# Expert rows loaded as 32x32 blocks and transposed by VectorE, zeros written at run-time addresses

## The chip, the cores and the metric

The kernel runs on one core of a Trainium2 chip. The time is the device time of one launch in microseconds (us). TensorE (PE) multiplies, VectorE (DVE), ScalarE (ACT) and GpSimd (POOL) do the rest, and SyncE (SP) issues most of the DMAs.

## The reference

Two stages follow one another. The first is a linear attention with a state (batch 4, 8 heads, 768 steps, head size 48):

```python
for t in range(S):
    kt, vt, rt = (k[:, :, t], v[:, :, t], r[:, :, t])
    cur = np.einsum('bhd,bhe->bhde', u[None] * kt, vt)
    y[:, :, t] = np.einsum('bhd,bhde->bhe', rt, state + cur)
    state = w[None, :, :, None] * state + np.einsum('bhd,bhe->bhde', kt, vt)
```

Its output, as 3072 tokens of 384 numbers, goes into a mixture of experts with 4 groups of 4 experts. Each token goes to one expert, the best of its best group:

```python
h = np.maximum(xg[mask_e] @ w1[g, e], 0.0)      # 384 -> 1024
ye = h @ w2[g, e]                               # 1024 -> 384
out[tok_idx] = (g_w[mask_g][mask_e] * e_w[mask_e])[:, None] * ye
```

All data is 32-bit float.

## The kernel before

**Attention stage.** The tokens are cut into 24 tiles of 128 (6 chunks of the sequence for each of 4 batches), and a loop over steps `s` runs a pipeline written out by hand: step `s` transposes tile `s` (`turn`), computes the scores of tile `s - 1`, the values of tile `s - 2`, brings tile `s - 3` back to rows (`back`) and finishes the routing of tiles further behind. The term of the token's own key (`own`, `own_sum`, `own_values`) runs on POOL, VectorE and ACT; `own_values(n)` makes eight scalings on ACT, which `back(n)` needs. The order of the instructions on each engine is the order of the code in this stage, since it is scheduled manually. The wait for data, on the other hand, is worked out by the framework: it sees a DRAM tensor that is addressed through a register as one whole.

**Routing.** After each group of tiles `route` picks an expert for every token and a place in that expert's region of the DRAM tensor `xs_dram` (named `x_sorted` in the profile). Each row there has 384 numbers, a token number and a gate. `rows` scatters 128 rows with an indirect DMA from POOL (L410). A region is longer than it has tokens, and the expert stage reads a fixed number of rows (`SLOTS`), so rows behind the last token must read as zeros. `zero_places` (L321) writes zeros over the first 256 places of every region in steps 3, 5, 7 and 9, in four DMAs from ACT's queue, ahead of all scatters.

**Expert stage.** After two thirds of the tiles `pick_first` names the two experts with most tokens; the others are sorted later (`order_i`). The experts run in that order, each with its number of slots, 256 for the first to 173 for the last. An item is one expert's work, the first expert being cut into two items. For item `i`: `load_rows` (L472) loads the rows from `xs_dram` in DMAs of up to 128 rows; `columns` (L483) transposes them on TensorE by blocks of 128x128 into PSUM and copies them to `xe` on VectorE (L486); `up` (L506) multiplies by w1, ACT applies relu (L510); `down` (L520) multiplies by w2; `rows_out` transposes back, multiplies by the gate and scatters to the output from POOL (L534). Two places hold weights, so `load_expert` (L430, L431) for w1 waits until `up` of two experts earlier is done, and for w2 until its `down` is done.

SP issues its DMAs strictly in order. In this stage the code of one item reads, cut to SP's share:

```python
up(i, 0); up(i, 2); up(i, 4); up(i, 6)
expert = expert_of(order_i[0:1, e : e + 1], (SP,))   # a register load
load_rows(i + 2, expert, nc.sync)
down(i, 0); columns(i + 1); down(i, 1); down(i, 2)
weights[e] = load_expert(expert, e % 2)
```

The DMAs of SP and ACT use eight semaphores in turn, so a DMA is not issued before the one eight places ahead of it has landed. Tiles of rows have three buffers.

Of the kernel before, what the change touches and what calls it, by code (L numbers as in the profile page):

```python
# [34 lines left out]
def kernel(  # L35
# [35 lines left out]

    x_dram = nc.dram_tensor("x_rows", [N, DM], FP32).ap()

    RG = N + P
    xs_dram = nc.dram_tensor("x_sorted", [GE * RG, XW], FP32).ap()
    w1f = moe_w1.rearrange("g e (ko p) f -> (g e) p ko f", p=P)
    w2f = moe_w2.rearrange("g e (fo p) d -> (g e) p fo d", p=P)
# [11 lines left out]
    def cst(shape, name, dtype=FP32):  # L89
        return const.tile(shape, dtype, name=name)  # L90
# [199 lines left out]

    is_first = cst([P, GE], "is_first")
    first_i = cst([P, 2], "first_i", I32)
    sorted_key = cst([P, GE], "sorted_key")
    order_i = cst([P, GE], "order_i", I32)

    def token_keys(i):

        pc = bank([P, 2, GE], "pc")
        nc.tensor.matmul(pc[:, 0, :], lhsT=ones, rhs=cum[:, i, :], start=True, stop=True)
        nc.vector.scalar_tensor_tensor(  # L300
            out=pc[:, 1, :], in0=pc[:, 0, :], scalar=float(GE), in1=key_base, op0=OP.mult, op1=OP.add
        )
        return pc[:, 1, :]

    def number_of(out, key_i):
        nc.vector.tensor_scalar(
# [3 lines left out]
    def pick_first():  # L310
        keys = token_keys(FOUR * B)
        top = cst([P, 8], "top")
        nc.vector.max(out=top, in_=keys)
        nc.vector.tensor_scalar(out=is_first, in0=keys, scalar1=top[:, 1:2], scalar2=None, op0=OP.is_ge)
        nc.vector.scalar_tensor_tensor(
            out=is_first, in0=keys, scalar=top[:, 0:1], in1=is_first, op0=OP.is_equal, op1=OP.add
        )
        nc.vector.tensor_copy(first_i, top[:, 0:2])
        number_of(first_i, first_i)

    def zero_places(j):  # L321

        regions = xs_dram.rearrange("(e n) w -> n e w", e=GE)
        part = CAP // 4
        nc.scalar.dma_start(out=regions[part * j : part * (j + 1)], in_=spread(nothing[0:part, :], 1, GE))

    NA = 1 + G

# [95 lines left out]
        ),  # L424
    ]

    def load_expert(e, i, queue=nc.sync):

        w1, w2 = places[i]
        queue.dma_start(out=w1, in_=w1f[bass.ds(e, 1)].rearrange("a p k f -> (a p) k f"))  # L430
        queue.dma_start(out=w2, in_=w2f[bass.ds(e, 1)].rearrange("a p k f -> (a p) k f"))  # L431
        return w1, w2

    def transposed(x, dst):

# [8 lines left out]


    ITEMS = [(0, 0, P), (0, P, SLOTS[0])] + [(e, 0, SLOTS[e]) for e in range(1, GE)]
    by_expert = xs_dram.rearrange("(e n) w -> e n w", e=GE)
    pools = {0: early}
    weights, xgs, xes, keys_of, hTs, yo = {}, {}, {}, {}, {}, {}

    def width(i):
        return ITEMS[i][2] - ITEMS[i][1]
# [7 lines left out]
    def room(i):  # L460
        return P if i == 0 else CAP

    def load_rows(i, expert, queue):
        shape = [P, room(i) // P, XW]
        if i < 3:
            xg = pools[0].tile(shape, FP32, name=f"xg_{i}")
        else:
            xg = pools[1].tile(shape, FP32, tag="xg", bufs=3, name="xg")
        xgs[i] = xg
        for j, n in enumerate(parts(i)):  # L470
            a = ITEMS[i][1] + P * j
            queue.dma_start(  # L472
                out=xg[0:n, j, :], in_=by_expert[bass.ds(expert, 1), a : a + n, :].rearrange("a n w -> (a n) w")
            )

    def columns(i):
        xg, w = xgs.pop(i), width(i)
        xe = xes[i] = item_tile(i, [P, KO, room(i)], "xe")
        for ks in (range(0, KO),) if KO * w <= 512 else (range(0, 2), range(2, KO)):
            px = bank([P, len(ks), w], "px")  # L480
            for q, ko in enumerate(ks):
                for j, n in enumerate(parts(i)):
                    nc.tensor.transpose(  # L483
                        px[:, q, P * j : P * j + n], xg[0:n, j, P * ko : P * (ko + 1)], ident[0:n, 0:n]
                    )
            nc.vector.tensor_copy(xe[:, ks[0] : ks[-1] + 1, 0:w], px)  # L486
        ids = item_tile(i, [P, 2], "ids", U32, bufs=4)
        gates = item_tile(i, [P, 2], "gates", bufs=4)
        for j, n in enumerate(parts(i)):
            nc.vector.tensor_scalar(  # L490
                out=ids[0:n, j : j + 1], in0=xg[0:n, j, DM + ROW_ID : DM + ROW_ID + 1], scalar1=float(N),
                scalar2=None, op0=OP.add,
            )
            nc.vector.tensor_copy(gates[0:n, j : j + 1], xg[0:n, j, DM + ROW_GATE : DM + ROW_GATE + 1])
        keys_of[i] = ids, gates

    def up(i, f):
# [186 lines left out]
    def expert_of(number, engines):  # L684
# [2 lines left out]
            skip_runtime_bounds_check_because="four bits of a whole number",  # L687
        )

    LAST = 5  # L690
    for s in range(NT + LAST):
        pieces = todo.pop(s, [])

        def run(when):
            for at, part in pieces:
                if at == when:
                    part()

        if s % 2 == 0 and s // 2 + 2 < NP:
            load_pair(s // 2 + 2)  # L700
        if s == 1:
            load_small()
        if s in (3, 5, 7, 9):
            zero_places(s // 2 - 1)
        if s == FOUR * B + 6:
            pieces.append(("last", pick_first))
        if s == FOUR * B + 7:
            first = expert_of(first_i[0:1, 0:1], (SP,))
            weights[0] = load_expert(first, 0)
        if s == FOUR * B + 9:  # L710
            load_rows(0, first, nc.sync)
            second = expert_of(first_i[0:1, 1:2], (SP,))
            weights[1] = load_expert(second, 1)
        if s == FOUR * B + 10:
            columns(0)
        run("first")
        if s < NT:
            turn(s)
            if s % 2 == 1 and s // 2 + 1 < NP:
                if s > 1:  # L720
                    scale_k(s // 2 + 1, nc.gpsimd)
                own(s // 2 + 1)
        for n in range(NT):
            if s == max(n + 1, 2):
                own_values(n)
        run("choice")
        if 0 <= s - 4 < NT:
            rows_T(s - 4)
        n = s - 5
        if 0 <= n < NT:  # L730
            row_logits(n)
        if 0 <= s - 3 < NT:
            back(s - 3)
        if 0 <= s - 2 < NT:
            values(s - 2)
        if s % 2 == 0 and 0 < s // 2 < NP:
            own_sum(s // 2)
        run("last")
        if 0 <= s - 1 < NT:
            scores(s - 1)  # L740
        if s == 1:
            own_sum(0)

        if s in (0, 3):
            backwards(s // 3 + 1, nc.scalar)
        if s in (1, 4):
            turned(s // 3 + 1)
            powers(s // 3 + 1, nc.scalar)
        if s == 3:
            span_decay()  # L750
        if s == 4:
            check_decay()
        if n in ROUTED:
            choice, before, gate, place, rows = routing(n)
            T = ROUTED[n]
            if n >= NT - B - 1:
                choice()
                todo.setdefault(s + 1, []).extend(
                    [("last", part) for part in (before, gate, place)]
                    + [("last", lambda i=i, rows=rows: rows(i)) for i in range(T)]  # L760
                )
            else:
                todo.setdefault(s + 1, []).append(("choice", choice))
                todo.setdefault(s + 2, []).extend([("first", before), ("last", gate), ("last", place)])
                for i in range(T):
                    at = s + 3 + (i // 2 if n == FOUR * B - 1 else i)
                    todo.setdefault(at, []).append(("last", lambda i=i, rows=rows: rows(i)))
        if s == FOUR * B + 10:
            up(0, 0)
# [12 lines left out]
    nc.vector.match_replace(out=keys, in_to_replace=sorted_key[:, 0:8], in_values=keys, imm_value=-1.0)  # L782
    nc.vector.max(out=sorted_key[:, 8:16], in_=keys)
    nc.vector.tensor_copy(order_i, sorted_key)
    number_of(order_i, order_i)
    over = cst([1, GE], "over")
    nc.vector.tensor_sub(over, sorted_key[0:1, :], most[0:1, :])
# [17 lines left out]
    with ExitStack() as moe:  # L805
        pools[1] = moe.enter_context(tc.tile_pool(name="moe", bufs=2, reuse_waits="tile"))
        with tc.manual_schedule(engines={mybir.EngineType.PE}):
            columns(1)
            for i in range(1, len(ITEMS)):
                up(i, 0)  # L810
                up(i, 2)
                if i > 1:
                    rows_out(i - 1)
                up(i, 4)
                up(i, 6)
                e = ITEMS[i][0] + 2
                if e < GE:
                    expert = expert_of(order_i[0:1, e : e + 1], (SP,))
                    load_rows(i + 2, expert, nc.sync)
                down(i, 0)  # L820
                if i + 1 < len(ITEMS):
                    columns(i + 1)
                down(i, 1)
                down(i, 2)
                if e < GE:
                    weights[e] = load_expert(expert, e % 2)
# [224 lines left out]
```

## Time and profile before

| what | value |
|---|---|
| median of 3 runs | 477.19 us (476.6 to 482.25) |
| the profiled execution | 479.58 us |
| its span, first to last instruction | 477.9 us |
| mean granted TensorE clock | 0.973 |
| TensorE busy | 449.7 us (94%) |
| VectorE, ACT, POOL busy | 159.5, 139.0, 129.5 us |
| DMA traffic | 86.24 MB, 112024 packets, mean 180 GB/s |

The span is that of the profiled execution. "Busy" is the time in which an engine runs instructions; an engine that waits or only issues DMAs is not busy. A line of a group gives the source line, engine, operation, output and inputs, shapes and count, then the total and the mean duration, and then the idle time before these instructions and who ended it. A line of the waits gives who waited, for whom, the total in us, the number of waits and the longest. A line of a timeline gives start and length in us, and in brackets the idle time before it. A line of a DMA issue gives the size and the median time from issue to landing.

### The profile page before, as it was taken

How to read it: one execution, taken by the hardware profiler on the slowest of the kernel's cores; microseconds unless marked ns; L12 is line 12 of the kernel's file. 1: busy time of each engine (PE TensorE's matmuls, PEld its weight loads, DVE VectorE, ACT ScalarE, POOL GpSimd, SP SyncE). 2: the span in 40 equal slices, each digit the busy share in tenths (PEclk: the TensorE clock that was granted, in tenths of full speed). 3: DMA queues.
4: the chain of work that ended last, by engine and by line, in shares of the span. 5: the costliest groups of instructions: out<-in, count | busy, mean ns of one | idle time of the engine just before them, and what ended most of it. 6: DMA issues, size and time to landing. Idle time of an engine off the chain costs nothing. (4 is left out here: it accounts for less than half of the span.)

```text
span 477.9 us, 9090 instructions
## 1 busy us (share of the span) xinstructions
PE 449.7 (94%) x3623; PEld 430.6 (90%) x3623; DVE 159.5 (33%) x478; ACT 139.0 (29%) x418; POOL 129.5 (27%) x135
## 2 busy tenths in 40 slices
PE   3799999999999898999999999999999999999992
PEld 2598888899999798999999999999999999999991
DVE  5546566877778663010110210110110110111000
ACT  2846553564656321111121111111111111111120
POOL 7834536556564042000010210110120110120011
PEclk9969979999999989999999999999999999999997
DMA  9999999983102994565465754755856765666000
GB/s 176 187 190 228 207 227 202 200 155 77 36 35 69 339 335 132 188 239 168 160 190 182 256 184 153 280 201 156 284 190 198 255 188 199 238 202 236 30 22 26
DMA packets 112024, 86.24 MB, mean 180 GB/s; under 512 B 79633, under 2 KB 103568, under 8 KB 111976
## 3 DMA queue, kind: packets, MB, share of 16 engines
q1 hardware_dynamic: 98920, 68.81, 52.1%
q10 hardware_dynamic: 8432, 7.31, 7.1%
q0 software_dynamic: 4624, 9.48, 5.8%
q8 instruction: 30, 0.49, 0.5%
q14 instruction: 18, 0.15, 0.1%
HBM read 69.79 MB, written 16.12 MB: 180 GB/s over the span
## 5 line engine op out<-in xcount | busy, mean ns | idle before, releaser
L534 POOL DMA_INDIRECT out_dram<-yt,ids x32 | 34.1, 1066 | 255.0 <-DVE yt L532 250.4
L506 PE MATMUL ph<-xe,w 128*128 128x128 f32 (+7 forms) x432 | 72.2, 325 | 0.7 <-DVE xe L486 0.7
L520 PE MATMUL po<-hT,w 128*128 128x128 f32 (+7 forms) x432 | 71.4, 322 | 0.0
L506 PEld LDWEIGHTS ph<-xe,w 128*128 128x128 f32 x432 | 69.0, 194 | 1.2 <-DVE xe L486 0.9
L532 DVE TENSOR_SCALAR yt<-pb,gates 128x384 f32<-128x384 f32 (+15 forms) x32 | 18.3, 611 | 153.4 <-PE pb L530 153.4
L520 PE MATMUL po<-hT,rall 128*128 128x240 f32 (+7 forms) x384 | 68.6, 336 | 0.0
L506 PE MATMUL ph<-xe,kall 128*128 128x240 f32 (+7 forms) x384 | 68.4, 335 | 0.0
L520 PEld LDWEIGHTS po<-hT,w 128*128 128x128 f32 x432 | 67.8, 190 | 0.5
L510 ACT ACTIVATE hT<-ph 128x256 f32<-128x256 f32 (+15 forms) x68 | 33.5, 493 | 112.9 <-PE ph L506 112.9
L520 PEld LDWEIGHTS po<-hT,rall 128*128 128x128 f32 x384 | 65.0, 190 | 0.7
L506 PEld LDWEIGHTS ph<-xe,kall 128*128 128x128 f32 x384 | 64.9, 190 | 0.6
L523 ACT COPY yo<-po 128x128 f32<-128x128 f32 (+15 forms) x51 | 16.3, 320 | 127.7 <-PE po L520 127.7
L564 ACT ACTIVATE dv<-vt,du 128x48 f32<-128x48 f32 x192 | 45.8, 324 | 1.1 <-DVE du L558 1.0
L594 DVE TENSOR_TENSOR am<-pa,later 128x512 f32<-128x512 f32 x48 | 30.9, 685 | 9.0 <-PE pa L589 8.7
L486 DVE COPY xe<-px 128x384 f32<-128x384 f32 (+30 forms) x32 | 14.0, 475 | 53.6 <-PE px L483 53.6
L410 POOL DMA_INDIRECT x_sorted<-xt,place_i x24 | 23.8, 990 | 27.9 <-issue 14.0
L589 PE MATMUL pa<-rT,kT 48*128 48x128 f32 x384 | 29.3, 291 | 0.7 <-DVE xt L646 0.7
L611 PE MATMUL py<-am,vt 128*64 128x128 f32 x384 | 29.2, 290 | 0.7 <-DVE am L594 0.6
L553 POOL TENSOR_TENSOR dg<-rall,kall 128x768 f32<-128x768 f32 x12 | 21.9, 1821 | 28.9 <-DVE du L558 28.9
L548 POOL TENSOR_TENSOR kh<-kall,T 128x768 f32<-128x768 f32 (+1 forms) x12 | 21.4, 1788 | 28.0 <-DMA kall<-in_k_dram 9.7
L611 PEld LDWEIGHTS py<-am,vt 128*64 128x64 f32 x384 | 22.7, 143 | 4.7 <-DVE am L594 1.5
L589 PEld LDWEIGHTS pa<-rT,kT 48*128 48x128 f32 x384 | 24.4, 193 | 2.6 <-DVE xt L646 0.9
(128 smaller groups left out, 469.6 us busy)
## 6 DMA issues: line engine op xcount, KB each, us to landing
w<-in_moe_w_dram SPq DMA_DIRECT2D x16, 1536.0 KB, 6.8
kall<-in_moe_w_dram SPq DMA_DIRECT2D x8, 1536.0 KB, 7.1
rall<-in_moe_w_dram SPq DMA_DIRECT2D x8, 1536.0 KB, 6.8
x_sorted<-nothing ACTq DMA_DIRECT2D x4, 1544.0 KB, 10.2
rall<-in_r_dram SPq DMA_DIRECT2D x12, 384.0 KB, 7.2
vt<-in_v_dram SPq DMA_DIRECT2D x12, 384.0 KB, 6.8
kall<-in_k_dram SPq DMA_DIRECT2D x10, 384.0 KB, 6.4
xg<-x_sorted SPq DMA_DIRECT2D x17, 193.0 KB, 6.2
```

Source lines behind the costliest of these rows:

```text
L410: ins = nc.gpsimd.indirect_dma_start(out=xs_dram, out_offset=bass.IndirectOffsetOnAxis(ap=place_i[:, i : i + 1], axis=0), in_=xt[:, i, :], ...
L506: nc.tensor.matmul(ph[:, q, :], lhsT=w1[:, ko, P * (f + q) : P * (f + q + 1)], rhs=xe[:, ko, 0:w], start=(ko == 0), stop=(ko == KO - 1), s ...
L510: nc.scalar.activation(hTs[i][:, f : f + 2, 0:w], ph, AF.Relu)
L520: nc.tensor.matmul(po, lhsT=w2[:, fo, P * d : P * (d + 1)], rhs=hT[:, fo, 0:w], start=(fo == 0), stop=(fo == FO - 1))
L532: nc.vector.tensor_scalar(out=yt[0:n], in0=pb[0:n], scalar1=gates[0:n, j : j + 1], scalar2=None, op0=OP.mult)
L534: ins = nc.gpsimd.indirect_dma_start(out=out, out_offset=bass.IndirectOffsetOnAxis(ap=ids[0:n, j : j + 1], axis=0), in_=yt[0:n], in_offset ...
L548: engine.tensor_mul(khs[g % (RING - 1)][:, a0:a1, :, 0:D], kts[g % RING][:, a0:a1], spread(T2[m], 1, a1 - a0))
L553: nc.gpsimd.tensor_mul(dg, rts[g % RING][:, :, :, 0:D], kts[g % RING])
L564: nc.scalar.mul(dv[:, h, :], vts[g % (RING + 1)][:, a, h, 0:D], dvs[g][:, a, h : h + 1])
L589: nc.tensor.matmul(pa[e][:, hc, :], lhsT=kT[rows, hc, :], rhs=rT[rows, hc, :], start=True, stop=True, skip_group_check=True,)
L594: nc.vector.tensor_mul(am[:, e], pa[e], spread(later, 1, HP))
L611: nc.tensor.matmul(py[DP * e : DP * (e + 1), hc, :], lhsT=vt[:, a, 2 * hc + e, :], rhs=am[:, e, hc, :], start=(c == 0), stop=True, skip_gr ...
```

## The change

The rows of an expert are no longer loaded as whole rows. Each item's tile is loaded by 12 DMAs, each of which takes 32 columns of all its tokens, in blocks of 32 tokens by 32 numbers (128 bytes at a time), so that each 32x32 block lies at the place where its transpose belongs; VectorE then transposes the blocks in place of TensorE. Token number and gate come with DMAs of their own (`key`). The four early zero fills are gone. In their place `no_tokens` writes zeros behind an expert's last token, at an address made of the count of its tokens, from SP's queue: for the first two experts after step 23 in the code, for every later one ahead of its row loads. Regions become 128 rows longer. The loads of the first two experts' weights are put in another order: w1 of the first, then rows and zeros, then the other three. `own_values(n)` runs one step later for n above 0. The four scatters of the sixteenth tile's group are put into one step.

```diff
-    def zero_places(j):
-        regions = xs_dram.rearrange("(e n) w -> n e w", e=GE)
-        part = CAP // 4
-        nc.scalar.dma_start(out=regions[part * j : part * (j + 1)], in_=spread(nothing[0:part, :], 1, GE))
+    regions = xs_dram.rearrange("(e n) w -> e n w", e=GE)
+    def no_tokens(e, count, rows):
+        for a in range(0, rows, P):
+            n = min(P, rows - a)
+            nc.sync.dma_start(out=xs_dram[bass.ds(e * RG + count + a, n), :], in_=nothing[0:n, :])
...
+        xg, key = xgs[i] = tl([P, KO, room(i)], "xg"), tl([P, room(i) // P, ROW_EXTRA], "key")
+        a, w, rows = ITEMS[i][1], padded(width(i)), regions[bass.ds(expert, 1)]
+        for q in range(P // BL):
+            for ko in range(KO):
+                col = P * ko + BL * q
+                queue.dma_start(
+                    out=xg[BL * q : BL * (q + 1), ko, 0:w].rearrange("t (b d) -> t b d", d=BL),
+                    in_=rows[:, a : a + w, col : col + BL].rearrange("a (b t) d -> t (a b) d", t=BL),
+                )
         for j, n in enumerate(parts(i)):
             queue.dma_start(
-                out=xg[0:n, j, :], in_=by_expert[bass.ds(expert, 1), a : a + n, :].rearrange("a n w -> (a n) w")
+                out=key[0:n, j, :], in_=rows[:, a + P * j : a + P * j + n, DM:XW].rearrange("a n w -> (a n) w")
             )
...
-            px = bank([P, len(ks), w], "px")
-            for q, ko in enumerate(ks):
-                for j, n in enumerate(parts(i)):
-                    nc.tensor.transpose(
-                        px[:, q, P * j : P * j + n], xg[0:n, j, P * ko : P * (ko + 1)], ident[0:n, 0:n]
-                    )
-            nc.vector.tensor_copy(xe[:, ks[0] : ks[-1] + 1, 0:w], px)
+        for ko in range(KO):
+            nc.vector.transpose(xe[:, ko, 0:w], xg[:, ko, 0:w])
...
         if s == FOUR * B + 7:
             first = expert_of(first_i[0:1, 0:1], (SP,))
-            weights[0] = load_expert(first, 0)
-        if s == FOUR * B + 9:
-            load_rows(0, first, nc.sync)
             second = expert_of(first_i[0:1, 1:2], (SP,))
-            weights[1] = load_expert(second, 1)
+            first_tokens = [tokens(first_n[0:1, i : i + 1]) for i in range(2)]
+            load_w1(first, 0)
...
-            if s == max(n + 1, 2):
+            if s == n + 2:
                 own_values(n)
...
+        if s == FOUR * B + 7:
+            load_rows(0, first, nc.sync)
+            no_tokens(first, first_tokens[0], CAP)
+            no_tokens(second, first_tokens[1], CAP)
+            load_w2(first, 0)
+            weights[0], weights[1] = places[0], load_expert(second, 1)
...
-                    at = s + 3 + (i // 2 if n == FOUR * B - 1 else i)
+                    at = s + 3 + (0 if n == FOUR * B - 1 else i)
...
                     expert = expert_of(order_i[0:1, e : e + 1], (SP,))
+                    no_tokens(expert, tokens(order_n[0:1, e : e + 1]), padded(SLOTS[e]))
                     load_rows(i + 2, expert, nc.sync)
```

`tokens` loads a count into a register of SP, and `padded` rounds up to a multiple of 32. `first_n` and `order_n` hold the counts, made by one shift each on VectorE.

More of the change, by code (lines that the diff above doesn't have):

```diff
@@ L72 @@
     x_dram = nc.dram_tensor("x_rows", [N, DM], FP32).ap()
-    RG = N + P
+    RG = N + CAP
     xs_dram = nc.dram_tensor("x_sorted", [GE * RG, XW], FP32).ap()
@@ L292 @@
     first_i = cst([P, 2], "first_i", I32)
+    first_n = cst([P, 2], "first_n", I32)
     sorted_key = cst([P, GE], "sorted_key")
     order_i = cst([P, GE], "order_i", I32)
+    order_n = cst([P, GE], "order_n", I32)
     def token_keys(i):
@@ L303, in token_keys, with tokens_of @@
         return pc[:, 1, :]
+    def tokens_of(out, key_i):
+        nc.vector.tensor_scalar(out=out, in0=key_i, scalar1=4, scalar2=None, op0=OP.logical_shift_right)
     def number_of(out, key_i):
@@ L318, in pick_first @@
         nc.vector.tensor_copy(first_i, top[:, 0:2])
+        tokens_of(first_n, first_i)
         number_of(first_i, first_i)
-    def zero_places(j):
-        regions = xs_dram.rearrange("(e n) w -> n e w", e=GE)
-        part = CAP // 4
-        nc.scalar.dma_start(out=regions[part * j : part * (j + 1)], in_=spread(nothing[0:part, :], 1, GE))
+    regions = xs_dram.rearrange("(e n) w -> e n w", e=GE)
[3 more added lines that the diff above has]
+            nc.sync.dma_start(out=xs_dram[bass.ds(e * RG + count + a, n), :], in_=nothing[0:n, :])
     NA = 1 + G
@@ L425, with load_w1, load_w2, load_expert @@
     ]
[L427 to L432, printed above, removed]
+    def load_w1(e, i):
+        nc.sync.dma_start(out=places[i][0], in_=w1f[bass.ds(e, 1)].rearrange("a p k f -> (a p) k f"))
+    def load_w2(e, i):
+        nc.sync.dma_start(out=places[i][1], in_=w2f[bass.ds(e, 1)].rearrange("a p k f -> (a p) k f"))
+    def load_expert(e, i):
+        load_w1(e, i)
+        load_w2(e, i)
+        return places[i]
     def transposed(x, dst):
@@ L446 @@
     ITEMS = [(0, 0, P), (0, P, SLOTS[0])] + [(e, 0, SLOTS[e]) for e in range(1, GE)]
-    by_expert = xs_dram.rearrange("(e n) w -> e n w", e=GE)
     pools = {0: early}
     weights, xgs, xes, keys_of, hTs, yo = {}, {}, {}, {}, {}, {}
+    BL = 32
     def width(i):
@@ L461, in room, with padded, tl @@
         return P if i == 0 else CAP
+    def padded(n):
+        return -(-n // BL) * BL
     def load_rows(i, expert, queue):
[L464 to L469, printed above, removed]
+        def tl(shape, name):
+            if i < 3:
+                return pools[0].tile(shape, FP32, name=f"{name}_{i}")
+            return pools[1].tile(shape, FP32, tag=name, bufs=3, name=name)
+        xg, key = xgs[i] = tl([P, KO, room(i)], "xg"), tl([P, room(i) // P, ROW_EXTRA], "key")
[7 more added lines that the diff above has]
+                )
         for j, n in enumerate(parts(i)):
-            a = ITEMS[i][1] + P * j
             queue.dma_start(
-                out=xg[0:n, j, :], in_=by_expert[bass.ds(expert, 1), a : a + n, :].rearrange("a n w -> (a n) w")
+                out=key[0:n, j, :], in_=rows[:, a + P * j : a + P * j + n, DM:XW].rearrange("a n w -> (a n) w")
             )
     def columns(i):
-        xg, w = xgs.pop(i), width(i)
+        xg, key = xgs.pop(i)
+        w = padded(width(i))
         xe = xes[i] = item_tile(i, [P, KO, room(i)], "xe")
-        for ks in (range(0, KO),) if KO * w <= 512 else (range(0, 2), range(2, KO)):
-            px = bank([P, len(ks), w], "px")
-            for q, ko in enumerate(ks):
-                for j, n in enumerate(parts(i)):
-                    nc.tensor.transpose(
-                        px[:, q, P * j : P * j + n], xg[0:n, j, P * ko : P * (ko + 1)], ident[0:n, 0:n]
-                    )
-            nc.vector.tensor_copy(xe[:, ks[0] : ks[-1] + 1, 0:w], px)
+        for ko in range(KO):
+            nc.vector.transpose(xe[:, ko, 0:w], xg[:, ko, 0:w])
         ids = item_tile(i, [P, 2], "ids", U32, bufs=4)
@@ L490, in columns @@
             nc.vector.tensor_scalar(
-                out=ids[0:n, j : j + 1], in0=xg[0:n, j, DM + ROW_ID : DM + ROW_ID + 1], scalar1=float(N),
-                scalar2=None, op0=OP.add,
+                out=ids[0:n, j : j + 1], in0=key[0:n, j, ROW_ID : ROW_ID + 1], scalar1=float(N), scalar2=None, op0=OP.add
             )
-            nc.vector.tensor_copy(gates[0:n, j : j + 1], xg[0:n, j, DM + ROW_GATE : DM + ROW_GATE + 1])
+            nc.vector.tensor_copy(gates[0:n, j : j + 1], key[0:n, j, ROW_GATE : ROW_GATE + 1])
         keys_of[i] = ids, gates
@@ L688, in expert_of, with tokens @@
         )
+    def tokens(number):
+        return nc.values_load(
+            number, engines=(SP,), min_val=0, max_val=N,
+            skip_runtime_bounds_check_because="no expert has more than all tokens",
+        )
     LAST = 5
@@ L702 @@
             load_small()
-        if s in (3, 5, 7, 9):
-            zero_places(s // 2 - 1)
         if s == FOUR * B + 6:
@@ L784 @@
     nc.vector.tensor_copy(order_i, sorted_key)
+    tokens_of(order_n, order_i)
     number_of(order_i, order_i)
```

## The prediction

> **What bounds the kernel now.** I read the page's busy shares first, then the groups by line and shape, the waits of SP's queue, SP's and TensorE's timelines, and the landing times of the DMAs. The busy shares, the groups of the expert stage and one stretch of the windows view:
>
> ```profile
> span 477.9 us, 9090 instructions
> PE 449.7 (94%) x3623; PEld 430.6 (90%) x3623; DVE 159.5 (33%) x478; ACT 139.0 (29%) x418; POOL 129.5 (27%) x135
> L483 PE MATMUL px<-ident,xg 128*128 128x128 f32 x51 | 12.2, 285 | 3.7 <-DMA xg<-x_sorted 3.7
> 300.00:350.00 50.00, 50.00 (x309) 49.82 (x308) 7.12 (x24) 8.53 (x20) 6.24 (x6) 1.00 0.63 215
> ```
>
> TensorE is the bound: in the expert stage it is busy in all 50 of 50 us at full clock, and VectorE works 7. Everything else is hidden as long as it comes in time. Whether it does is read from SP, which issues all loads in a fixed order:
>
> ```profile
> SPq L431 <- PE po L520: 117.0, 14, 9.8
> SPq L430 <- PE ph L506: 93.7, 14, 7.9
> SPq L472 <- DMA x_sorted<-xt,place_i: 27.6, 6, 16.4
> ...
> 163.12 0.35 SPq L472 DMA_DIRECT2D xg<-x_sorted  x1
> 164.49 0.38 SPq L430 DMA_DIRECT2D kall<-in_moe_w_dram  x1
> 165.12 0.37 SPq L431 DMA_DIRECT2D rall<-in_moe_w_dram  x1
> 184.23 2.96 SPq L472 DMA_DIRECT2D xg<-x_sorted  x5
> 193.55 0.39 SPq L430 DMA_DIRECT2D w<-in_moe_w_dram  x1
> 199.55 0.38 SPq L431 DMA_DIRECT2D w<-in_moe_w_dram  x1
> 200.70 0.86 SPq L472 DMA_DIRECT2D xg<-x_sorted  x2
> ...
> w<-in_moe_w_dram SPq DMA_DIRECT2D x16, 1536.0 KB, 6.8
> DMA to landing us min/median/max: 2.4/6.2/7.6
> ...
> 168.76 0.97 POOL L410 DMA_INDIRECT x_sorted<-xt,place_i  x1 [12.59 <-DMA xg<-x_sorted]
> 168.09 0.52 PE L483 MATMUL px<-ident,xg 128*128 128x128 f32 x3 [3.00 <-DMA xg<-x_sorted]
> ```
>
> Per expert SP waits about 15 us for TensorE (117.0 + 93.7 over 14): that is its slack. A cycle is: w2 of one expert when down is done (199.55), the next rows at once (200.70), then w1 when up is done, then w2. From w2 to w2 it takes 20.4 us for the widest expert and 17.0 for the narrowest (SP's timeline); TensorE sets it. A row load alone lands in 2.4 us, behind a w2 in 6.2 (the last line but two is of the row loads). And two places around 165 us are tight: POOL's scatter waits 12.59 us for a row load to finish, TensorE waits 3.00 us for it.
>
> **What the skill says.** "DMA: Bandwidth & Descriptors", section "Queues, rings and completion order": on each DMA engine the descriptors of SP's row are consumed in ring order. The 6.2 against 2.4 us agree: rows issued 1.15 us after w2 land just after it. The same page, "Latency and other measured facts", gives about 600 ns as the floor of a register load; here one takes 0.3 to 0.5, which I use. "VectorE: DVE Perf Modes", "The three transpose paths": 311 ns for a 128x128 VectorE transpose of 2-byte data, in 32x32 blocks; no run here shows one yet. "TensorE: Matmul & The Clock Gate", part 1: after an idle window of 3.4 us the clock is halved; after the 3.00 us wait the same 12 matmuls of L506 took 2.47 us, later 1.58, so it agrees.
>
> **The change part by part.**
>
> Removed from TensorE: 96 transposes of xg (L483). From the first of each group to the next other instruction it is 0.5 to 0.6 us per expert, 1.3 in the last five, 0.35 and 1.17 for the two halves of the first: 13.7 us in all, all of it on the path today. With them go 32 PSUM copies of 0.475 us (VectorE, hidden).
>
> Added on VectorE: 51 block transposes. Nearest row: the 128x384 copy, 0.56 us, so 0.2 to 0.5 each; three per item are about 1.2 us beside 17 us of matmuls: nothing. For item 0 they stand in front of routing work, but xe was copied there before too.
>
> Own terms one step on: ACT then has 8 instead of 16 scalings (0.24 us apart) ahead of the first yT at 21.08, which can come 1.9 us sooner. TensorE next waits for am at 22.97 and that hangs on the du reduction of POOL's product, unmoved. Gain 0 to 2 us; I take 0. The four zero fills of 1544 KB leave ACT's queue (10 us each to landing). kh waited once 9.7 us on a k load beside them, but no TensorE wait follows from it: 0 to 3, I take 0.
>
> Moved and added on SP, the transition. The order is now: four register loads (0.4 each), w1 of the first expert, 12 block loads and one key load for xg_0, four zero writes each waiting for the one before (same tensor, address unknown to the scheduler), then w2, w1, w2. Before, first_i was known at 151.76. With three more register loads w1 goes at about 153.9. The last of the 16 early scatters is issued at 155.2. It landed at 162.9 behind two weight loads; with one ahead I take 160.3. Row loads are 0.56 apart (five with one register load take 2.96), so the thirteenth goes at 167.1 and lands at 169.4. Columns and up(0,0) follow at about 170.3 against 170.5 before: no loss. Then four zeros at about 2.6 each (lower bound 2.4, the lone row load; upper 3.5): 172, 174.6, 177.2, 179.8. w2 of the first expert is issued at 177.8 instead of 153.06. POOL's last eight scatters, which waited for the row load until 168.76, now wait for the fourth zero, 179.9. They are 1.28 apart: last at 188.9 instead of 181.3. They share the engines with three weight loads, so w2 lands at about 187 and TensorE, due for down(0,0) at 179.74, stands 7 us. The last scatter lands near 194.5; only then come the 13 loads of xg_1, in the ring behind the weights: 194.6 + 12 x 0.56 + 2.4 = about 203.7. up(1) starts at 204 instead of 187.89: 16 us lost. SP is through xg_1 and xg_2 (28 loads with keys) at 210.3; expert 2's zeros (issue, two landings) take till 216.8 and 14 row loads till 224.9, when its w1 is issued.
>
> Added on SP per expert, the cycle: a second register load, two zero writes one behind the other, 12 block loads and 2 key loads for 2 row loads. Behind these stand w1 and w2 of the same expert. Run back to back, from w1's issue: w2 at 0.6; first zero issued at 2.1 (w2 to rows is 1.15 today, plus a load), but in the ring behind 3 MB of weights. One weight load lands in 6.8; the second adds 4.9 (6.8 less the 2.4 of a lone small load, plus its 0.5 of data), so the zero lands at 12.0. The second zero is issued then and lands 2.65 later: 14.65. Fourteen loads at 0.56: 7.85. Next w1 at 22.5. The 128-byte blocks, some 2800 an expert, cost the engines little: the r, k, v loads have 2048 packets of 192 bytes each and SP passes one in about 2.0 us, so 256 blocks need 0.26 of the 0.56.
>
> 22.5 is more than TensorE's 17 to 20. Items 2 to 4 still run on weights loaded ahead; from item 5 TensorE waits for w1, 3 us and then 5 to 6 each time. Half clock after such a wait stays inside the longer cycle.
>
> **The sum.** Expert 2's w1 at 224.9, expert 15's 13 cycles later: 224.9 + 13 x 22.5 = 517.4. The last item starts 6.3 after (w1 in), 523.7; its down ends at about 538.5 (14.8 today, from 452.6 to 467.4); from there to the end it is 10.5 us today: 549. The profiled execution lies 1.7 us above its span (479.58), and the median of the runs 2.4 below that, 477.19. One half-clock window in the last item adds about 1.7. I take 550.
>
> **Rivals.**
>
> Small blocks dear (chance 0.11): each block load takes 1.0 us of SP, or the engines 60 ns a block; the packets' records of the r, k, v loads, 15 to 19 ns each, speak against it, nothing in the trace shows 128-byte reads of HBM. Cycle 28.6: 225 + 13 x 28.6 + 32 = 629.
>
> SP's slack holds (0.07): the other side, not slower. The zeros do not stand behind the weights, landing 2.5 after their issue. Then from w2: 1.5 + 2.5 + 2.65 + 7.85 = 14.5, below the 17 of TensorE. It decides at a cycle of about 17; the 15 us of slack speak for it, the 6.2 us landing of rows behind w2 against it. 477.9 + 16 - 13.7 + 1.7 - 2.4 = 480, within 2%.
>
> Clean gain (0.04): the same, and the transition's zeros and scatters overlap too: 477.2 - 13.7 - 3 = 460.
>
> **How the numbers follow.** 0.78 for the forecast. Its range: zeros and issue at their low ends, cycle 20.5 and start 220, give 220 + 266.5 + 31.5 = 518; at the high ends, cycle 25.5 and start 229, 592. With the neighbours' weight I give 512 to 597. 2% is about what a measurement of this kernel can tell from no change: slower 0.89, same 0.07, faster 0.04.
>
> **What would show it.** Right: SP's w1 issues evenly 21 to 24 us apart from about expert 4; TensorE waits at ph for the weight DMA, not for xe; half-clock digits in the expert stage; POOL waiting for zeros until about 180. The step is wrong if zeros land 2.5 us after issue while weights are in the ring, if block loads are not about 0.56 apart, or if TensorE stays at 50 of 50.

## The result, and the profile after

The changed kernel takes 537.18 us (median, 535.63 to 537.73) against 476.89 for the kernel before on the same chip: a ratio of 1.1222, 95% interval 1.115 to 1.1294. Ratios and intervals, here and below, leave out runs more than 1.5% above the fastest of their kernel, and the plain quotient of the two medians (1.1264 here) differs from them by up to 0.7%, inside each interval. The profiled execution takes 536.7 us, its span is 535.0. Against the span of before, 477.9, that is 57.1 more. Lines of the page, and the windows view of the same stretch as the prediction shows of before:

```profile
span 535.0 us, 9759 instructions
PE 458.4 (86%) x3527; PEld 440.4 (82%) x3527; DVE 164.1 (31%) x499; ACT 139.1 (26%) x418; POOL 129.8 (24%) x135
L527 PE MATMUL ph<-xe,kall 128*128 128x240 f32 (+7 forms) x384 | 81.6, 378 | 26.8 <-DMA kall<-in_moe_w_dram 21.6
L527 PE MATMUL ph<-xe,w 128*128 128x128 f32 (+7 forms) x432 | 80.4, 349 | 20.8 <-DMA w<-in_moe_w_dram 12.5
L508 DVE STREAM_TRANSPOSE xe<-xg 128x224 f32<-128x224 f32 (+3 forms) x51 | 18.6, 385 | 112.6 <-DMA xg<-x_sorted 112.0
x_sorted<-nothing SPq DMA_DIRECT2D x19, 193.0 KB, 8.5
xg<-x_sorted SPq DMA_DIRECT2D x96, 28.0 KB, 2.0
300.00:350.00 50.00, 46.15 (x259) 45.35 (x257) 7.13 (x25) 7.28 (x17) 3.89 (x4) 0.97 0.65 197
```

TensorE lost the 96 transposes (3623 to 3527 instructions), yet it is no longer full: 46.15 of 50 us in the stretch, 86% of the span. The idle time stands ahead of `up` (L527) and was for the most part ended by the loads of w1, called `kall` or `w`. The mean of one matmul went up as well, from 325 to 349 ns for `w`, since half-clock stretches follow most of these waits: in the TensorE timeline below 24 matmuls take 6.22 us after a wait of 4.11 us, and the next 24 of the same item take 4.47. Who keeps the weights is read from SP: first its waits, then its timeline through one item, then TensorE's timeline beside it.

```profile
SPq L333 <- DMA x_sorted<-nothing: 106.6, 17, 8.4
SPq L494 <- DMA x_sorted<-nothing: 24.2, 14, 2.5
SPq L439 <- PE po L541: 0.5, 2, 0.3
...
303.92 0.41 SPq L436 DMA_DIRECT2D w<-in_moe_w_dram  x1
304.57 0.40 SPq L439 DMA_DIRECT2D w<-in_moe_w_dram  x1
306.25 9.16 SPq L333 DMA_DIRECT2D x_sorted<-nothing  x2
317.18 6.01 SPq L494 DMA_DIRECT2D xg<-x_sorted  x12
323.44 0.86 SPq L499 DMA_DIRECT2D key<-x_sorted  x2
324.86 0.41 SPq L436 DMA_DIRECT2D kall<-in_moe_w_dram  x1
...
289.95 6.22 PE L527 MATMUL ph<-xe,kall 128*128 128x212 f32 x24 [4.11 <-DMA kall<-in_moe_w_dram]
310.74 4.42 PE L527 MATMUL ph<-xe,w 128*128 128x206 f32 x24 [1.01 <-DMA w<-in_moe_w_dram]
331.20 6.02 PE L527 MATMUL ph<-xe,kall 128*128 128x202 f32 x24 [2.84 <-DMA kall<-in_moe_w_dram]
```

SP's wait for TensorE, 210.7 us over the stage before (the 117.0 and 93.7 in the prediction's lines), is down to 0.8: the 0.5 shown and 0.3 for `up`. It now waits for its own zeros. The first is issued at 306.25, the second about 8.8 us later, and the first block load 2.1 us after that. From one w1 to the next there are 20.9 us here, in which TensorE needs about 17. So from the item that starts at 290.0 on each item starts with a wait for weights.

The passage from the attention stage to the experts, on SP's and then TensorE's timeline:

```profile
155.79 6.43 SPq L494 DMA_DIRECT2D xg<-x_sorted  x12
164.08 6.77 SPq L333 DMA_DIRECT2D x_sorted<-nothing  x4
171.04 0.41 SPq L439 DMA_DIRECT2D w<-in_moe_w_dram  x1
...
179.00 8.24 PE L541 MATMUL po<-hT,w 128*128 128x128 f32 x48 [5.42 <-DMA w<-in_moe_w_dram]
196.13 4.18 PE L527 MATMUL ph<-xe,w 128*128 128x128 f32 x18 [8.20 <-DVE xe L508]
```

w2 goes out at 171.04 instead of 153.06, and TensorE waits 5.42 us for it and later 8.20 us for the rows of item 1. The whole loss divides cleanly. The first matmul on `kall` (the start of item 2) is at 209.5 instead of 199.4: 10.2 us. From there to the end of the last `down` it is 315.1 us (to 524.6) instead of 268.2 (to 467.5): 46.9 us. The 10.3 us behind it are the same in both. 10.2 + 46.9 = 57.1.

### The profile page after: what moved, and what is told of

The parts are those of the page before. It is cut to its first block, busy times and chain, and to the rows that moved or that the text cites. A ratio compares the mean times of both kernels' runs of the same rounds, so it can differ in the third digit from the quotient of the medians.

```text
span 535.0 us, 9759 instructions
## 1 busy us (share of the span) xinstructions
PE 458.4 (86%) x3527; PEld 440.4 (82%) x3527; DVE 164.1 (31%) x499; ACT 139.1 (26%) x418; POOL 129.8 (24%) x135
## 5 line engine op out<-in xcount | busy, mean ns | idle before, releaser
L527 PE MATMUL ph<-xe,kall 128*128 128x240 f32 (+7 forms) x384 | 81.6, 378 | 26.8 <-DMA kall<-in_moe_w_dram 21.6
L527 PEld LDWEIGHTS ph<-xe,kall 128*128 128x128 f32 x384 | 77.2, 222 | 29.2 <-issue 28.4
L527 PE MATMUL ph<-xe,w 128*128 128x128 f32 (+7 forms) x432 | 80.4, 349 | 20.8 <-DMA w<-in_moe_w_dram 12.5
L527 PEld LDWEIGHTS ph<-xe,w 128*128 128x128 f32 x432 | 76.2, 213 | 23.1 <-issue 20.9
L541 PEld LDWEIGHTS po<-hT,w 128*128 128x128 f32 x432 | 70.7, 199 | 5.8 <-issue 5.5
L541 PE MATMUL po<-hT,rall 128*128 128x240 f32 (+7 forms) x384 | 67.0, 334 | 0.0
L508 DVE STREAM_TRANSPOSE xe<-xg 128x224 f32<-128x224 f32 (+3 forms) x51 | 18.6, 385 | 112.6 <-DMA xg<-x_sorted 112.0
L632 PE MATMUL py<-am,vt 128*64 128x128 f32 x384 | 27.7, 280 | 2.7 <-DVE am L615 2.6
L632 PEld LDWEIGHTS py<-am,vt 128*64 128x64 f32 x384 | 21.3, 137 | 6.5 <-DVE am L615 3.4
L600 ACT COPY kT<-pk 128x512 f32<-128x512 f32 x24 | 14.0, 585 | 35.2 <-PE pk L596 35.2
```

What stands on the lines that cost most here:

```text
L508: nc.vector.transpose(xe[:, ko, 0:w], xg[:, ko, 0:w])
L527: nc.tensor.matmul(ph[:, q, :], lhsT=w1[:, ko, P * (f + q) : P * (f + q + 1)], rhs=xe[:, ko, 0:w], start=(ko == 0), stop=(ko == KO - 1), s ...
L541: nc.tensor.matmul(po, lhsT=w2[:, fo, P * d : P * (d + 1)], rhs=hT[:, fo, 0:w], start=(fo == 0), stop=(fo == FO - 1))
L632: nc.tensor.matmul(py[DP * e : DP * (e + 1), hc, :], lhsT=vt[:, a, 2 * hc + e, :], rhs=am[:, e, hc, :], start=(c == 0), stop=True, skip_gr ...
```

## The experiments

The theory: the block loads and the zeros are each affordable, but together they make SP's chain per item longer than TensorE's work, and its largest piece is a zero that queues behind the 3 MB of weights issued just before it. The rivals: the small blocks are dear in themselves; a write to HBM is slow wherever it stands; one of the smaller edits costs time. Each ratio is against the kernel before, measured beside the experiment on the same chip; its medians there were 478.77, 481.50 and 479.24 us.

**Own terms alone.** The kernel before, with one line of the change:

```diff
-            if s == max(n + 1, 2):
+            if s == n + 2:
                 own_values(n)
```

> The kernel before with one edit: own_values runs one step later. The changed kernel's attention stage was 6.8 us shorter than before (22nd tile's transposes at 131.7 us, not 138.6). Theory: the shift does it. ACT has 8 scalings in place of 16 ahead of the first yT, TensorE's long wait near 20 us shortens, and the half-clock stretch after it (22.3 to 32.5 us) with it: 472 to 475 us, 22nd tile at 133 to 136. Rival: the four zero fills that left the stage do it; then this kernel stays within 1 us of before, 22nd tile at 138 to 139. Second rival: only the chance of the clock's windows; then 138.6 with other half-clock stretches.

478.95 us, ratio 1.0002 (0.9975 to 1.003), so the 472 to 475 us that the shift should have brought are missed. TensorE's 2.9 us wait at 21.7 became one of 2.4 us at 23.0, for `am`, and the 22nd tile starts at 137.9 us. The edit is worth nothing by itself.

**The early fills put back** into the changed kernel:

```diff
+        if s in (3, 5, 7, 9):
+            zero_places(s // 2 - 1)
```

> The changed kernel with the four zero fills of 1544 KB put back on ACT's queue in steps 3, 5, 7 and 9 (all else, the late zeros too, stays). Theory that the shift of own_values shortened the attention stage: 537 us as without them, 22nd tile at 131 to 133 us. Rival that the fills cost it: 541 to 545 us, 22nd tile at 136 to 140.

540.3 us, ratio 1.1319 (1.126 to 1.1378), against the change's own 1.1222. The intervals overlap: from the ratios the fills cost some 5 us, and anything between nothing and some 9 us is in keeping with both intervals. The 22nd tile starts at 133.1 us, short of the 136 to 140 that the rival asked for. What the profiles say of them follows with the point on the attention stage below.

**Blocks alone**: the kernel before with the change's `load_rows` and `columns`, the early fills, the old order of weights, and no zeros from SP.

```diff
+        for q in range(P // BL):
+            for ko in range(KO):
...
+        for ko in range(KO):
+            nc.vector.transpose(xe[:, ko, 0:w], xg[:, ko, 0:w])
```

> The kernel before with block loads, key loads and VectorE transposes alone; zeros stay the four early fills, weights stay in their old order. Theory: SP is bound by the chain of loads, zeros and waits together, not by the blocks. From w2 SP needs 1.2 + 14 loads of 0.52 + a wait for w2 to land, about 10 us, below TensorE's 17: no waits for weights, 13.7 us of transposes gone, about 4 to 8 us lost where 13 loads stand ahead of the first two items: 467 to 473 us. Rival: the 12 small loads are the cost in themselves; then TensorE waits for weights per expert and the time is above 500 us.

474.17 us, ratio 0.991 (0.9874 to 0.9946), 1 us above what was expected. The windows view of this kernel:

```profile
300.00:350.00 50.00, 50.00 (x300) 49.91 (x299) 6.77 (x27) 8.86 (x21) 6.26 (x6) 1.00 0.70 208
```

TensorE is full, and items 2 to 16 take 255.8 us instead of 268.2: the removed transposes bring 12.4. But item 2 starts at 208.4 instead of 199.4. Waits of 4.2 us (at 170.6) and 5.0 us (at 195.9, for `xe`) show that the rows of the first items come too late. Item 0's 12 block loads take 7.3 us to issue there, and a VectorE transpose of such an item only 0.31. So the blocks are not dear in the stage, and they take back most of their gain in the passage.

**Zeros alone**: the changed kernel with row loads, TensorE's transposes and the old own step.

```diff
-            nc.vector.transpose(xe[:, ko, 0:w], xg[:, ko, 0:w])
+                    nc.tensor.transpose(
+                        px[:, q, P * j : P * j + n], xg[0:n, j, P * ko : P * (ko + 1)], ident[0:n, 0:n]
+                    )
```

> The changed kernel with whole-row loads and TensorE transposes as before, own_values at its old step; the zeros behind each expert's tokens and the new order of the first weights stay. Theory: cycle per expert = 0.65 (w2) + 1.7 + 9 (first zero behind the weights) + 2.2 (second) + 2 x 0.55 = 14.7 us, still below TensorE's 17: the expert stage stays at full TensorE busy, only the transition loses 8 to 12 us: 482 to 490 us. Rival: the zeros' waits alone are the bound; then TensorE waits for weights in every item and the time is above 505 us.

480.63 us, ratio 1.0038 (1.0016 to 1.0061), less than the 482 to 490 expected. SP's waits, its timeline through one item, and the window:

```profile
SPq L439 <- PE po L537: 65.5, 14, 9.1
SPq L333 <- DMA x_sorted<-nothing: 36.8, 17, 5.1
...
313.44 0.38 SPq L333 DMA_DIRECT2D x_sorted<-nothing  x1
314.02 0.38 SPq L436 DMA_DIRECT2D w<-in_moe_w_dram  x1
316.01 0.36 SPq L333 DMA_DIRECT2D x_sorted<-nothing  x1
...
300.00:350.00 50.00, 50.00 (x308) 49.82 (x307) 7.13 (x24) 8.73 (x20) 6.24 (x6) 1.00 0.72 226
```

SP still has slack (65.5 us of waiting for TensorE), and TensorE is full. But SP's order is not that of the changed kernel: in the last ten of the 14 pairs of zeros w1 is issued between the two and w2 behind them, here at 319.53, so the first zero has no weights issued just ahead of it. The run shows that zeros fit beside row loads in this order; it does not price them in the changed kernel's order. Blocks cost -0.9% and zeros +0.4%; both together cost 12%. The costs don't add: each uses up a part of the 15 us of slack per item, and only together do they go past it. In the changed kernel's cycle the two zeros take 11.0 us and the 14 loads 8.2 (the table below), where two row loads took 0.9 before: some 18 us more.

**Blocks only where there is slack**: the kernel before with rows for items 0 to 2, blocks from item 3 on, early fills, own terms one step on.

```diff
     def load_rows(i, expert, queue):
+        if i >= 3:
+            return load_blocks(i, expert, queue)
```

> The kernel before with blocks, key loads and VectorE transposes for items 3 to 16 only; the first three items keep whole-row loads and TensorE transposes, zeros stay the four early fills, own_values one step later. Theory: the blocks alone won 12.3 us from item 2 on and lost 9.0 where 13 loads stood ahead of the first two items; without those the loss goes: 478.8 - 11.7 = 465 to 468 us, last down ending near 456 us. Rival: the loss at the start came from something else in the block form (VectorE's transposes, the pools), and the gain is hidden by SP's chain, which then shows as waits for weights: 474 us as with blocks for all items.

468.52 us, ratio 0.9755 (0.9712 to 0.9799), half a us above what was expected and faster than both kernels. Item 2 starts at 197.9, and items 2 to 16 take 255.8 us again. So both halves of the reading of "blocks alone" hold: the gain of 12.4 is in the stage, the loss was in the passage, with the blocks of the first three items.

**Later zeros on ACT's queue**, ahead of each item's `up`:

```diff
-                    no_tokens(expert, tokens(order_n[0:1, e : e + 1]), padded(SLOTS[e]))
...
+                    no_tokens(
+                        expert_of(order_i[0:1, e : e + 1], (ACT,)), tokens(order_n[0:1, e : e + 1], (ACT,)),
+                        padded(SLOTS[e]), nc.scalar,
+                    )
```

> The changed kernel with the later experts' zero writes issued from ACT's queue, at the start of an item in program order, so that they stand neither in SP's ring behind the weights nor in SP's order; the four first zeros stay on SP. Theory: the first zero's 8 to 9 us behind 3 MB of weights is what makes SP's cycle longer than TensorE's. Then a zero lands 2 to 4 us after its issue, SP needs about 10 to 14 us per expert, and TensorE bounds: 536 - 60 = 473 to 485 us. Rival: the waits between zeros, rows and zeros are long wherever they are issued; then row loads still wait for zeros and the time stays above 515 us.

517.93 us, ratio 1.0822 (1.0747 to 1.0897): the theory's number is missed by far. The timeline of ACT, then one of its waits:

```profile
303.04 6.77 ACTq L333 DMA_DIRECT2D x_sorted<-nothing  x2
309.85 0.57 ACT L544 COPY yo<-po 128x212 f32<-128x212 f32 x2 [9.60 <-DMA x_sorted<-nothing]
...
ACT yo L544 <- DMA x_sorted<-nothing: 76.6, 13, 9.6
```

The second zero is issued about 6.4 us after the first (5.6 to 6.5 in 13 items, 6.1 in the mean), so the first still takes most of its time. In the trace's packet records the first packet of such a zero goes out 3.4 to 4.1 us after its issue. With no weights in flight it is 0.87 us, on either queue. On SP's queue, in the changed kernel, it is 5.1 to 7.3 us, 6.9 in the mean, and the last packet of w2 goes out 7.2 to 8.3 us after the zero's issue. My idea that the delay belongs to SP's ring alone was wrong: leaving the ring took away about half of it. A zero can be issued only when the rows before it have landed, and by then SP has issued the weights, whichever queue the zero takes: w1 went out 0.8 to 4.6 us ahead of it in these 13 items. The Trainium skill ("DMA: Bandwidth & Descriptors", "Issuing engines are not separate DMA queues") says that DMAs of all issuing engines run on the same 16 DMA engines and interleave. The zero's packets that run beside w2's, in all 13 items, agree. Why its first packet still takes over 3 us is not explained by it, and I leave it open. The new place also stops ACT behind the zero (76.6 us in all). The cycle shrank from 21.8 to 19.9 us only.

**One write instead of two** per expert, of the same bytes:

```diff
-        for a in range(0, rows, P):
-            n = min(P, rows - a)
-            nc.sync.dma_start(out=xs_dram[bass.ds(e * RG + count + a, n), :], in_=nothing[0:n, :])
+        n = rows // 2
+        nc.sync.dma_start(
+            out=xs_dram[bass.ds(e * RG + count, rows), :].rearrange("(p a) w -> p a w", a=2),
+            in_=spread(nothing[0:n, :], 1, 2),
+        )
```

> The changed kernel with one zero write of all rows in place of two writes one behind the other (each piece of the zero tile is written twice); everything else as changed. Theory of a serial chain: a cycle of 21.8 us becomes 21.8 - 2.3 = 19.5, times 13, and the transition's two waits of 2.1 go too: 537 - 26 to 34 = 503 to 511 us, w1 issues 19 to 20 us apart. Rival: what counts is the data in the ring, not the number of waits; then 530 us or more.

517.32 us, ratio 1.0753 (1.0699 to 1.0808): the right direction, less than expected. SP's timeline:

```profile
299.55 0.66 SPq L332 DMA_DIRECT2D x_sorted<-nothing  x1
308.59 6.02 SPq L496 DMA_DIRECT2D xg<-x_sorted  x12
```

From the zero's issue to the first block load it is 9.0 us here and 9.75 in the mean over 13 items, against 8.71 + 2.33 = 11.04 for the two writes. Taking away the second landing saves 2.33, but the single write with both parts' bytes takes 1.0 longer. The cycle went from 21.78 to 20.68.

**Fewer weights.** The theory's own test: the changed kernel, with most of the weights of experts 2 to 15 left out of the loads (which its time must be read with), and every other instruction in place.

```diff
-                    weights[e] = load_expert(expert, e % 2)
+                    nc.sync.dma_start(out=w1[:, 0:1], in_=one[:, 0:1])
+                    nc.sync.dma_start(out=w2[:, 0:2], in_=two[:, 0:2])
```

> The changed kernel with most of the weights of experts 2 to 15 left out: one of three blocks of w1 and two of eight of w2 are loaded, 512 and 384 KB instead of 1,536 and 1,536 KB; every other instruction stands. Theory (the 8 to 9 us from the first zero's issue to its landing are the time in which the weights issued just before it leave the ring): 896 KB leave it in about 3 us, so the first zero lands 2.5 to 5 us after its issue, an item's chain on SP shrinks from 21.8 to 15.5 to 17 us, TensorE's 17 us bound again, no waits for weights are left, 476 to 485 us. Rival (a write to HBM at a register's address takes its 8 us whatever lies ahead of it in the queue): the first zero still lands 7 us or more after its issue, the cycle stays at 20 us or more, 515 us or more.

477.62 us, ratio 0.9977 (0.9956 to 0.9998). SP's waits, its timeline and the window:

```profile
SPq L333 <- DMA x_sorted<-nothing: 33.7, 17, 2.8
SPq L861 <- PE po L541: 13.3, 7, 3.6
...
303.08 2.52 SPq L333 DMA_DIRECT2D x_sorted<-nothing  x2
...
300.00:350.00 50.00, 50.00 (x299) 49.91 (x298) 6.64 (x20) 9.07 (x21) 6.24 (x6) 1.00 0.43 107
```

With 0.9 instead of 3 MB ahead of it the first zero takes 2.1 to 3.5 us until the next is issued, and the wait for zeros falls from 106.6 to 33.7 us. SP waits for TensorE again, TensorE is full, and items 2 to 16 take 255.8 us, as with blocks and no zeros from SP. The start of item 2 is where the change has it, 209.3. So the 59.3 us between 315.1 and 255.8 go with the weights, while all zeros and all small loads are still there. In the changed kernel 39.3 of them are TensorE's waits at `up`, and the other 20 are longer matmuls, in half-clock stretches; they fit inside SP's longer cycle. The packet records say where the zero's time went: its first packet goes out 0.9 to 1.5 us after the issue here, for 5.1 to 7.3 in the changed kernel. The rival of a slow write is out.

Not run alone were the new order of the first experts' weights and the four scatters put into one step, so what each of them has in the 10.2 us of the passage stays open.

## Why the prediction was right, and where its sizes were off

**The mechanism held.** SP's serial chain binds, not TensorE, and the zeros queue behind the weights. TensorE waits for w1 from item 6 on, one item later than forecast, by 1.0 to 7.0 us where the prediction had 3 and then 5 to 6. The prediction's cycle against the means of 13 items in SP's timeline:

| step on SP | predicted us | measured us |
|---|---|---|
| w1 to w2 | 0.6 | 0.74 |
| w2 to the first zero | 1.5 | 1.86 |
| first zero to second zero | 9.9 | 8.71 |
| second zero to first block load | 2.65 | 2.33 |
| 14 loads, to the next w1 | 7.85 | 8.15 |
| sum | 22.5 | 21.78 |

The step that was too large is the first zero's: I let the second weight load add 4.9 us to the 6.8 of one. From w1's issue to the second zero's that gave 12.0 us, and 11.3 were measured, which is 9 us in 13 cycles. The other steps nearly cancel, and 13 cycles were 9.3 us shorter than I had them.

**The term that fell outside its bounds is the attention stage**, taken as 0. w1 of the first expert went at 147.12, where I had 153.9, and everything behind it came 7 to 8 us early: expert 2's w1 at 217.07 for 224.9. The stage was 6.8 us shorter, more than both edits' bounds (0 to 2 and 0 to 3) together. The start of the 22nd tile, less half of the half-clock time ahead of it, is at 130.0 to 132.8 in the five profiles with early fills, and at 127.5 to 129.0 in the five without; the means are 131.4 and 128.2. That gives the fills some 3 us of stalls: argued from these profiles, while the times of the run with the fills put back neither prove nor refute it. For this pair of profiles it is 1.7 us by that measure (130.0 to 128.3). The other 5.1 are half-clock stretches, 17.1 us of them before and 6.8 after. They differ from one profile to the next (3.4 to 17 us), so this part of the miss is chance as far as the profiles tell.

What starts the half-clock stretches is not settled. In the expert stage of the changed kernel one follows each of the eight waits of 2.33 us and more, and none follows the three of 2.27 us and less. In the attention stage of before one starts at 66.7, with a single wait of 0.73 us close ahead of it, while the run with the fills put back has the same wait (0.74) and none behind it. So the length of one wait does not decide it, and the 3.00 us wait of the kernel before, shorter than the 3.4 us window that the prediction quotes, is no evidence for that window.

**The passage was sized rightly, by parts that cancel.** up(1) starts at 196.13 against 187.89 before; with the 6.8 us gained ahead of it that is 15.1 lost, for 16 predicted. From w1's issue to w2's it took the 23.9 us predicted, but the first zero came 1.5 us later in it (17.0 for 15.5), and a lone zero took 2.1 us instead of 2.6 (four in 6.77 with the last's issue). TensorE stood 5.4 us for w2, not 7, and POOL's next scatter went at 174.0 instead of 179.9.

**The end.** From the last w1 at 500.25 to the end of the span it is 34.7 us, where I had 31.6 and 1.7 apart for one half-clock window; the last item's w1 was in 6.9 us after its issue (6.3 predicted), and its first 24 matmuls, in a half-clock stretch, took 6.24 us where they took 3.68 before. Together, against the predicted span of 549: -7.8 (start), -9.3 (cycles), +3.1 (end) = 535.0.

**Costs taken as nothing.** The VectorE transposes take 385 ns in the mean (0.2 to 0.5 estimated). The six of 128x128 take 312 in the mean, next to the 311 ns that the Trainium skill ("VectorE: DVE Perf Modes", "The three transpose paths") gives for 2-byte data of this size. VectorE is busy 7.13 of 50 us, so they are hidden. Own terms one step on: nothing, as the run shows.

**The rivals.** "Small blocks dear": a block load is issued every 0.51 us and lands in 2.0; blocks alone are 0.9% faster. "SP's slack holds" gave 480 us if zeros landed 2.5 us after issue: with the weights cut the zeros do that (2.1 to 3.5), and 477.62 were measured. So that sum came near, though it has no gain in the attention stage, and its condition was wrong for the kernel as changed. The removed transposes, put at 13.7 us, brought 12.4 from item 2 on wherever TensorE is the bound.

## What to carry to other kernels

Slack on an issuing queue is a budget that several edits share: check the sum of all of them against the period of the bound, not each by itself. In an in-order queue, price a wait for a DMA by what has been issued just ahead of it, not by its own bytes: here 193 KB took 2.1 us alone and 8.7 behind 3 MB. Moving such a DMA to another queue helped only in part here (6.1 us), since it was still issued just behind the large loads; and a finer load that pays in the steady stage may be held back at the stage's start, where nothing covers it.

## What the runs showed of the hardware that I had not expected

Reads of HBM in 128-byte packets were cheap: 14 ns a packet in the trace's records, so 256 of them over 16 DMA engines need an estimated 0.22 us, less than the 0.51 us that SP needs to issue the load. And a zero on ACT's queue, with w1 and w2 in flight on SP's, began 3.4 to 4.1 us after its issue, for 0.87 us with none in flight, though the queues are different. The Trainium skill ("DMA: Bandwidth & Descriptors", "Queues, rings and completion order") has the engines take turns between queues packet by packet. That agrees with what came after the first packet: in nine of the 13 items packets of the zero went out before w1's last one, in four of these 76 to 126 of its 128, and w2's ran beside it in all. The 3.4 to 4.1 us ahead of the first packet are not accounted for by it.
